# A two-layer spectral and dense network on one core: fewer filler products, the first rows in quarters, and vector work moved between steps

## The chip, the cores and the metric

The kernel runs on one core of a Trainium2 chip. The metric is the device time of one execution in microseconds (us); the median of several executions counts. The engines are PE (matmuls; its weight loads are listed as PEld), DVE (vector), ACT (activation functions, copies), POOL and SP. Each runs its own stream of instructions in order and waits for the others by semaphores. SP, ACT and POOL also issue the transfers (DMAs).

## The reference

Two kinds of layer, A and B, are applied in turn, twice: A, B, A, B. x is 2048 x 1024 in bf16.

```python
def _layernorm(x, axis=-1, eps=1e-5):
    m = jnp.mean(x, axis=axis, keepdims=True)
    v = jnp.var(x, axis=axis, keepdims=True)
    return (x - m) / jnp.sqrt(v + eps)

def _A_ref(x, w_r, w_i):                      # a filter in the frequency domain
    X = jnp.fft.rfft2(x.astype(jnp.float32), axes=(-2, -1))
    X = X * (w_r + 1j * w_i)
    return jnp.fft.irfft2(X, s=(S, D), axes=(-2, -1)).astype(jnp.bfloat16)

def _B_ref(x, w1, b1, w2):                    # w1 is 1024 x 3584, w2 is 3584 x 1024
    h = jnp.einsum("bsd,df->bsf", x, w1) + b1
    act = h * jnp.tanh(softplus(h))           # softplus is written out in full there
    return jnp.einsum("bsf,fd->bsd", act, w2)

x = x + _A_ref(_layernorm(x), A_w_r, A_w_i)
x = x + _B_ref(_layernorm(x), B_w1, B_b1, B_w2)
x = x + _A_ref(_layernorm(x), A_w_r, A_w_i)
x = x + _B_ref(_layernorm(x), B_w1, B_b1, B_w2)
```

## The kernel before, in words

x stays on the chip as `XS`, 16 tiles of 128 tokens. A Python class records each engine's instructions in the order of the calls and works out the semaphore waits; nothing is reordered. So the order in which the code calls its helpers is the order on each engine. `Res` objects keep track of who wrote and who read a buffer; a transfer that fills part of a buffer is put down to the `Res` of that part, and a reader waits for all transfers of that `Res`.

**The start.** `prologue` issues on the SP queue: the 16 tiles of x, small constants, and a second copy of x with the axes turned (`XR`), which the first stage of A reads as its stationary operand. Each of the 24 transfers of `XR` takes one eighth of the columns and some rows, in runs of 256 bytes: 8 transfers for rows 0 to 63 (`xr0`), 8 for rows 64 to 95, 8 for rows 96 to 127. Behind them on the queue are the tables `FD` and `JT`, the filter rows of the groups 0 and 1 (`load_wr`), and more tables. `first_scales` works out the scale of each token (DVE, ACT), and `scaled(j)` multiplies a constant matrix by the scales of one group of 8 row pairs, on DVE or POOL (L615) or, for j = 1, on ACT in 8 instructions (L609).

**A.** `s1` is the first stage: 16 groups of 8 matmuls (L634), four to a quarter of `XR`, each evicted by ACT (L640) or DVE (L642). Then `order_A` lists the rest of A by hand, as three-digit words: stage, group, half. Stage 2 (`s2`, L741) is a transform that ACT (L776) or DVE (L778) evicts; in the first A `filter_bins` (L1032 on PE, L1043 on DVE, L1047 on ACT) follows some of these words and prepares the filter. Stage 3 (`s3`, L786 to L789) is the next transform: ACT scales it (L798), DVE multiplies by the filter in four instructions (L800 to L807). Stages 4 and 5 (`i1`, L842, and `i2`, L872 and L904) go back; ACT evicts them (L858, L916), and the rows are written to DRAM (`u_turn`) and read back turned (`u_back`, `u_last`) for the last stage `i4` (L1071). The last rows, of group 7, are read back in four transfers, two on ACT's queue and two on SP's; a part of `i4` waits for the one that holds its rows.

While those rows travel, PE runs filler: `spin` (L651, real operands, result unused), `residual_first` (L1060, puts the old x into PSUM) and `hold` (L656), which adds n products with a zero matrix to a bank, so that the bank's value stays. `hold` is called with 16 (first A) or 11 (second A) ahead of `i4`, and once more with 2 after its first part.

**B, first product, start.** B works on four chunks of 512 tokens (4 tiles). `mm1(c, fg, half)` (L1220) multiplies chunk c, or half of it, by two blocks of 128 columns of w1: 8 matmuls each into one of three PSUM banks in rotation, which ACT evicts with Mish (L1224). Between those calls stand the residual sums of the tiles (`residual(j)`, DVE, L1498), the statistics for the layer norm, either on DVE (L470, L473) or on ACT (`stats_act`: two passes over a tile, Copy and Square, with a running sum, both L451; DVE's `sums_to_mv` from L462 on turns the sums into mean and variance), the scales, `apply` (L522, the normalised tile) and the transposes by PE (L1181) with DVE's copies (L1186).

**B, the Strassen-like parts.** The chunks 0 and 1, then 2 and 3, are multiplied by seven products each instead of eight. `quads` does that for the first matrix, one step per pair of w1 blocks: products by PE (L1260), the sums by DVE (`add`, L1265), Mish by ACT (L1270), copies of a shared product by ACT (L573, in `block`); `corner` finishes one of the quarters. After each step it calls `after(n)`, a list of things to do in step n: loads, statistics, scales, `normal(j)` (apply and transpose by DMA) and residual sums. In the second B (`last`), some blocks and corners come ahead of `quads`. `products` does the second matrix (L1359), with DVE's sums (L1402, L1410).

The layers are joined with no barrier: what one layer's last steps release is what the next layer waits for.

## Time and profile before

| what | value |
|---|---|
| median of 3 executions | 928.98 us (928.76 to 930.48) |
| the profiled execution: its own time | 925.04 us |
| its span, first to last instruction | 923.2 us |
| granted TensorE clock | 1.000 |
| PE busy | 877.7 us, 95% of the span |
| DVE, ACT, POOL busy | 623.4, 435.0, 147.7 us |
| chain that ended last, PE's share | 88% |
| costliest groups on PE | L1359 340.1 us, L1260 280.4 us, L1220 73.4 us |

In the profile a line like L1260 is the line of the kernel that issued the instruction. "ARENA" and "PS" are the on-chip buffer and PSUM, "XS" is x. A timeline line begins with the start and the duration in us; a bracket at its end is the idle time of the engine before it and what ended it. Times of the second half of the kernel are counted from the same start: the first A runs to about 117 us, the first B to 474, the second A to about 564, and the second B to the end.

### The profile page before, as it was taken

The numbers are of one execution on the slowest core, as the hardware profiler recorded it, in microseconds if no ns is written. First come the engines' busy times: TensorE is split into PE (matmuls) and PEld (weight loads), VectorE is DVE, ScalarE is ACT, GpSimd is POOL, SyncE is SP. The second block draws the span as 40 slices with busy tenths as digits, with TensorE's granted clock in tenths as the row PEclk, the third lists the DMA queues.
The fourth block names the chain that finished last, engine by engine and source line by source line (L and its number), as shares of the span: only waits on it lengthen the run. The fifth ranks groups of instructions, "written<-read, shape, count | busy, mean of one in ns | idle before, by whom it ended". The sixth has DMA issues, their size and how long they took to land.

```text
span 923.2 us, 13610 instructions
## 1 busy us (share of the span) xinstructions
PE 877.7 (95%) x5503; PEld 471.1 (51%) x5503; DVE 623.4 (68%) x995; ACT 435.0 (47%) x645; POOL 147.7 (16%) x170
## 2 busy tenths in 40 slices
PE   0899889999999999999998998999999999999998
PEld 0677576444444444444456766754444444444443
DVE  7798468686889667568767765676747655554463
ACT  7898485456203485420018966757540025552000
POOL 0732004960004651010121200000000000000000
PEclk9999999999999999999999999999999999999999
DMA  9979861575786388364723786345166645732432
GB/s 279 284 249 287 219 194 67 210 266 139 262 281 239 131 317 298 121 233 143 281 92 114 221 217 161 137 175 184 23 197 189 204 148 180 269 121 86 173 129 102
DMA packets 153502, 175.98 MB, mean 191 GB/s; under 512 B 75000, under 2 KB 132568, under 8 KB 153320
## 3 DMA queue, kind: packets, MB, share of 16 engines
q1 hardware_dynamic: 140256, 130.32, 45.9%
q0 software_dynamic: 10032, 42.90, 12.5%
q10 hardware_dynamic: 3152, 1.90, 0.7%
q8 instruction: 43, 0.70, 0.3%
q14 instruction: 19, 0.16, 0.0%
HBM read 130.78 MB, written 40.89 MB: 186 GB/s over the span
## 4 chain that ended last, share of the span: by engine, by line
PE 88%; DVE 6%; ACT 3%; SPq 2%; DMA 1%; issue 0%; DVEq 0%
PE PS L1359 37%; PE PS L1260 30%; PE PS L1220 6%; PE PS L741 3%; PE PS L842 2%; PE PS L872 2%; SPq L251 2%; PE PS L1071 2%; PE PS L634 1%; PE PS L651 1%; ACT ARENA L640 1%; PE PS L1181 1%; PE PS L904 1%; PE PS L1060 1%; ACT ARENA L451 1%; PE PS L656 1%
## 5 line engine op out<-in xcount | busy, mean ns | idle before, releaser
L1359 PE MATMUL PS<-ARENA 128*128 128x512 bf16 x1568 | 340.1, 379 | 0.0
L1260 PE MATMUL PS<-ARENA 128*128 128x512 bf16 (+1 forms) x1288 | 280.4, 379 | 0.8 <-DVE ARENA L1265 0.8
L1359 PEld LDWEIGHTS PS<-ARENA 128*128 128x128 bf16 x1568 | 153.3, 98 | 184.5
L1265 DVE TENSOR_TENSOR ARENA<-PS,ARENA 128x512 f32<-128x512 f32 x230 | 157.1, 691 | 100.2 <-PE PS L1260 92.4
L1260 PEld LDWEIGHTS PS<-ARENA 128*128 128x128 bf16 x1288 | 125.3, 98 | 153.3 <-DVE ARENA L1265 3.6
L1270 ACT ACTIVATE ARENA<-ARENA,B 128x512 bf16<-128x512 f32 x138 | 98.8, 721 | 69.1 <-DVE ARENA L1265 63.8
L573 ACT ACTIVATE ARENA<-PS 128x512 f32<-128x512 f32 (+3 forms) x86 | 61.6, 726 | 110.6 <-PE PS L1260 92.5
L1153 POOL TENSOR_TENSOR ARENA<-ARENA 128x512 bf16<-128x512 bf16 x56 | 71.5, 1278 | 74.3 <-DVE ARENA L522 61.1
L451 ACT ACTIVATE ARENA<-XS 128x1024 bf16<-128x1024 bf16 x60 | 63.2, 1053 | 36.6 <-DVE XS L1410 33.0
L1220 PE MATMUL PS<-ARENA 128*128 128x256 bf16 (+1 forms) x528 | 73.4, 295 | 3.4 <-DVE ARENA L1186 1.9
L1384 DVE TENSOR_TENSOR ARENA<-ARENA 128x3584 bf16<-128x3584 bf16 x32 | 63.9, 2017 | 0.0
L1410 DVE TENSOR_TENSOR XS<-PS,ARENA 128x512 bf16<-128x512 f32 x52 | 35.7, 689 | 39.0 <-PE PS L1359 38.7
L1220 PEld LDWEIGHTS PS<-ARENA 128*128 128x128 bf16 x528 | 50.3, 98 | 22.3 <-DVE ARENA L1186 3.3
L1402 DVE TENSOR_TENSOR ARENA<-PS,ARENA 128x512 f32<-128x512 f32 x48 | 32.9, 688 | 28.0 <-PE PS L1359 27.6
L1224 ACT ACTIVATE ARENA<-PS,B 128x256 bf16<-128x256 f32 (+1 forms) x66 | 33.0, 515 | 29.0 <-PE PS L1220 28.8
L1270 ACT ACTIVATE ARENA<-PS,B 128x512 bf16<-128x512 f32 x46 | 31.5, 685 | 18.4 <-PE PS L1260 18.4
L1398 DVE TENSOR_TENSOR ARENA<-ARENA,XS 128x512 f32<-128x512 f32 x52 | 36.8, 731 | 0.5
L442 ACT ACTIVATE RS<-MV,EPS 128x1 f32<-128x1 f32 (+2 forms) x11 | 3.3, 296 | 71.5 <-DVE MV L564 70.1
L741 PE MATMUL PS<-FD,ARENA 128*128 128x256 bf16 (+1 forms) x256 | 31.4, 271 | 2.5 <-ACT ARENA L640 2.5
L842 PE MATMUL PS<-ARENA 128*128 128x256 bf16 x256 | 32.6, 273 | 1.0 <-DVE ARENA L807 0.6
L798 ACT ACTIVATE ARENA<-PS 128x1024 bf16<-128x1024 f32 x30 | 30.4, 1046 | 5.0 <-PE PS L789 5.0
L1235 DVE TENSOR_TENSOR ARENA<-ARENA 128x2048 f16<-128x2048 bf16 x16 | 25.3, 1583 | 9.0 <-PE PS L1220 8.7
(102 smaller groups left out, 811.4 us busy)
## 6 DMA issues: line engine op xcount, KB each, us to landing
ARENA<-in_B_w_dram SPq DMA_DIRECT2D x30, 896.0 KB, 6.7
ARENA<-w1s_scratch SPq DMA_DIRECT2D x28, 896.0 KB, 4.7
ARENA<-w2s_scratch SPq DMA_DIRECT2D x24, 896.0 KB, 6.6
w1s_scratch<-ARENA POOLq DMA_DIRECT2D x14, 896.0 KB, 4.6
ARENA<-in_B_w_dram SPq DMA_DIRECT2D x24, 512.0 KB, 4.3
u_scratch<-ARENA SPq DMA_DIRECT2D x14, 512.0 KB, 4.9
ARENA<-u_scratch SPq DMA_DIRECT2D x14, 512.0 KB, 6.0
w2s_scratch<-ARENA POOLq DMA_DIRECT2D x8, 896.0 KB, 4.1
```

The lines of the kernel that those rows point to most:

```text
L451: self.op(act, lambda e, i=i, f=f: e.activation(junk.ap, x, f, accum_out=sums[:, i:i + 1]), reads=[self.r_xs[j]], writes=[junk.res], parts ...
L573: fn = (lambda e: e.activation(dst, src, ACT.Copy)) if scale is None else \
L741: fns.append(lambda e: e.matmul(dst, at(r), FD[:, t:t + n], start=start, stop=stop))
L842: fns.append(lambda e, c=c, part=part: e.matmul(ps[:, c * 256:(c + 1) * 256], yk.ap[:, part, c * P:(c + 1) * P], t[:, (128, 0)[part]:(384, ...
L1153: self.op(self.pool, lambda e, dst=A(dst), x=A(x), y=A(y), op=op: e.tensor_tensor(dst, x, y, op), reads=[b.res] + list(after), writes=[b.rs])
L1220: fns.append(lambda e, db=db, bank=bank, fl=fl: e.matmul(PS[:, bank, 0:w], wb.ap[:, db, fl * P:(fl + 1) * P], x.ap[:, db, tok], start=(db ...
L1260: self.group([lambda e, db=db: e.matmul(PS[:, bank, :], A[:, db, :], mov[:, db, :], start=(start and db == 0), stop=(db == 3), skip_group_ ...
L1265: self.op(dve, lambda e: e.tensor_tensor(dst.ap, PS[:, bank, :], x.ap, ALU.add), reads=[self.r_bank[bank], x.res], writes=[dst.res])
L1270: self.op(act, lambda e: e.activation(at, src, ACT.Mish, bias=self.B1[:, ft:ft + 1]), reads=[res, self.r_b1], writes=[ra])
L1359: self.group([lambda e, i=i, k=k, b=PB[n][k].ap: e.matmul(PS[:, bank, :], ap[:, i, t * P:(t + 1) * P], b[:, i - 7 * k, :], start=(start an ...
L1384: self.op(dve, lambda e: e.tensor_tensor(ap[dst][:, f, :], ap[x][:, f, :], ap[y][:, f, :], op), reads=part(x, k) + part(y, k), writes=part ...
L1398: self.op(dve, lambda e: e.tensor_tensor(a[t], a[t], x, ALU.add), reads=[rx], writes=[r[t]])
```

## The change

It has five parts. (1) `XR` is loaded in four quarters of 32 rows, 32 transfers instead of 24, and a group waits for its own quarter. (2) In `order_A` the word 221 moves ahead of 400. (3) `hold` ahead of `i4` runs 12 products instead of 16 in the first A, and 5 instead of 11 in the second. (4) `stats_act` can do one of its two passes; the four passes for the tiles 6 and 7, until now two after `mm1(0, 1, 1)` and two after `mm1(0, 2, 1)`, come one after each of `mm1(0, 1, 1)`, `mm1(0, 2, 1)`, `mm1(0, 3, 1)`, and the last one after `mm1(0, 4)` in the first B or after `corner(1, 4)` in the second. (5) In `quads` of the second B the residual sums of the tiles 12 and 13 are made in steps 1 and 3 instead of both in step 7; those of 14 and 15 stay in steps 8 and 9, and the first B keeps its steps.

```diff
-        for q, n in ((0, 2), (2, 1), (3, 1)):
+        for q in range(4):
             r = Res(f"xr{q}")
             for h in range(8):
-                s = slice(32 * q, 32 * (q + n))
+                s = slice(32 * q, 32 * q + 32)
                 self.dma(sp, self.XR.ap[h:P:8, s, :], xv[h][:, s, :], f"xr{q}", parts=[r])
-            self.r_xr += [r] * n
+            self.r_xr.append(r)
...
-    def stats_act(self, j):
+    def stats_act(self, j, passes=(0, 1)):
         act = self.act
         x, sums, rs, junk = self.XS[:, j, :], self.BN[:, j, 0:2], self.r_mv[j], self.junk
-        rs.begin()
-        for i, f in enumerate((ACT.Copy, ACT.Square)):
+        if passes[0] == 0:
+            rs.begin()
+        for i in passes:
+            f = (ACT.Copy, ACT.Square)[i]
...
-        self.hold(11 if li else 16, 7)
+        self.hold(5 if li else 12, 7)
...
-        order = ("200 201 210 211 300 301 220 310 400 221 311 401 230 320 410 500 231 321 411 501 330 331 420 510 240 511 421 241 "
+        order = ("200 201 210 211 300 301 220 310 221 400 311 401 230 320 410 500 231 321 411 501 330 331 420 510 240 511 421 241 "
...
         for fg in range(1, 4):
             mm1(0, fg, 1)
-            if fg < 3:
-                self.stats_act(5 + fg)
+            self.stats_act(6 + fg // 3, ((fg - 1) % 2,))
         if not last:
             mm1(0, 4)
+            self.stats_act(7, (1,))
...
             corner(1, 4)
+            self.stats_act(7, (1,))
             turns(1, 0)[0]()
...
-            for j in {first + 1: (12, 13), first + 2: (14,), first + 3: (15,)}.get(n, ()):
+            late = {1: (12,), 3: (13,), 8: (14,), 9: (15,)} if last else {5: (12, 13), 6: (14,), 7: (15,)}
+            for j in late.get(n, ()):
                 residual(j)
```

## The prediction

> **What bounds the kernel now.** I read the page first (engine shares, chain), then the waits of PE, then PE's timeline around each place that the diff touches, and last the timelines of the engine named as releaser.

> ```profile
> span 923.2 us, 13610 instructions
> ...
> PE 877.7 (95%) x5503; PEld 471.1 (51%) x5503; DVE 623.4 (68%) x995; ACT 435.0 (47%) x645; POOL 147.7 (16%) x170
> ...
> PE 88%; DVE 6%; ACT 3%; SPq 2%; DMA 1%; issue 0%; DVEq 0%
> ```

> PE is busy 95% of the span and is 88% of the chain. No edit removes useful matmuls, so all that can be won is idle time of PE, and filler that stands where PE could start real work. The waits of PE (total, times, longest, in us) name the idle time:

> ```profile
> PE PS L634 <- DMA ARENA<-in_A_x_dram: 2.7, 1, 2.7
> ...
> PE PS L1220 <- ACT ARENA L1224: 1.4, 3, 0.6
> ...
> PE PS L1260 <- DVE ARENA L1265: 0.8, 1, 0.8
> ...
> PE PS L842 <- DVE ARENA L807: 0.6, 1, 0.6
> ```

> Each of these four is the target of one edit. PE's timeline shows where they lie (start, duration; idle before and releaser in brackets), with the filler L656 of the first layer:

> ```profile
> 23.97 7.87 PE L634 MATMUL PS<-ARENA 128*128 128x128 bf16 x80 [2.73 <-DMA ARENA<-in_A_x_dram]
> ...
> 107.25 3.66 PE L656 MATMUL PS<-BD,ARENA 128*128 128x512 bf16 x16
> 110.92 0.95 PE L1071 MATMUL PS<-MT,ARENA 128*128 128x32 bf16 x32
> ...
> 139.53 2.77 PE L1220 MATMUL PS<-ARENA 128*128 128x256 bf16 x16 [0.62 <-ACT ARENA L1224]
> 142.47 3.63 PE L1220 MATMUL PS<-ARENA 128*128 128x512 bf16 x16 [0.17 <-ACT ARENA L1224]
> ...
> 498.55 1.05 PE L842 MATMUL PS<-ARENA 128*128 128x256 bf16 x8 [0.64 <-DVE ARENA L807]
> ...
> 586.83 1.05 PE L1220 MATMUL PS<-ARENA 128*128 128x256 bf16 x8 [0.61 <-ACT ARENA L1224]
> ...
> 659.48 2.76 PE L1260 MATMUL PS<-ARENA 128*128 128x512 f16 x12 [0.78 <-DVE ARENA L1265]
> ```

> Matmuls overlap, so the bracket understates what is lost; I take the start-to-start step of the matmuls (0.109 us for 256 columns, 0.216 for 512) and count what exceeds it.

> [...]The trace shows the half rate at the start (L634 steps 0.107 us from 23.97 to 29.9, then 0.056) and shows that PE keeps the full rate after a gap of 1.16 us before 38.11 and 1.30 us before 491.00 (L741 steps 0.109). [...]Mish evictions L1224 whose matmuls are done wait behind L451. [...]between 13 and 31 us the DMA share is 1.23 to 1.30 at 213 to 236 GB/s[...].

> **The change part by part.**

> *Rows in quarters.* The first half of the transposed x comes now as 8 transfers of 256 KB, the last issued at 18.67 and landing 5.2 us later, at 23.9: PE starts at 23.97. As quarters, PE needs 8 of 128 KB. The first 256 KB landed at 15.25 and the rest at some 0.62 us per 128 KB, so the first quarter is there by about 19.6 and the new bound is the scaled matrices: L615 of group 0 ends at 22.77, the 8 L609 of group 1 at 24.12. Group 1 then starts at 24.15, not 24.80: 0.65 gained. The second quarter (wait added before group 4; all later groups queue behind it on PE) should land at about 24.6, needed at 26.7. From 30.1 on, ACT's L640 evictions pace the groups, and the end of the stage moves from 38.0 to about 37.4. Then the cover ends: PE's L1032 (39.59) needs filter rows whose last transfer is issued at 32.87 on the same SP queue and lands 6.3 us later, 39.2. SP issues 8 transfers more: 16 at 0.67 instead of 8 at 1.2, about 1.1 us more in the unblocked part[...]. From 13.86 I get 26 x 0.67 = 17.4 us, to 31.3, against 31.09: 0.2 late. So L1032 could start at 39.45: a gain of 0.1. POOL's filter loads wait for the same stage (37.26), start 0.6 earlier, and compete with those rows. I take 0; bounds -0.6 (nothing late next) and +0.8 (all 1.1 us of issue felt, less 0.35 of slack before L1032).

> *Order of A.* `221` before `400`. In the second A, PE ends s3 (1,0) at 497.74 and waits for L807 until 498.55. The s2 group of 8 matmuls (0.87 us) fits there; i1 (0,0) then starts at 498.62, not before its data (498.50), and s3 (1,1) at 499.5 instead of 500.30: 0.8. The next i1 (0,1) needs DVE's second product, done at 500.5, so it starts at 500.55 and not 501.17: 0.62 remains, and PE runs without a longer wait to 539.8. On ACT the eviction of `221` goes ahead of that of `400`; the s3 eviction behind both moves up with PE. Gain 0.6, bounds 0 to 0.8. In the first A, DVE is busy without a break from 42.04 to 60.4 and paces the stage; its order is unchanged: 0.

> *Zero products.* First layer: 16 become 12, PE would be free 4 x 0.216 = 0.86 us earlier, at 110.05. But L1071 reads u rows issued by ACT at 107.51, 3.2 us to landing: 110.7. Gain 0.2; the next reads, issued at 108.17 and landing 3.7 later (111.87), just match. Second layer: 11 become 5, PE free at 557.1 instead of 558.37; rows issued at 553.82 plus 4.1 land at 557.93. Gain 0.4; the next rows (554.46 + 4.6 = 559.06) are needed at 559.2. Sum 0.6, bounds 0 and 2.15 (all 10 products).

> *Statistics of tiles 6 and 7.* Each tile is two ACT passes L451 of 1.15 us start to start. Two together hold back the Mish that frees PE's bank:

> ```profile
> 136.79 1.06 ACT L451 ACTIVATE ARENA<-XS 128x1024 bf16<-128x1024 bf16 x1
> ...
> 137.97 1.06 ACT L451 ACTIVATE ARENA<-XS 128x1024 bf16<-128x1024 bf16 x1
> ...
> 139.02 0.82 ACT L1224 ACTIVATE ARENA<-PS,B 128x256 bf16<-128x256 f32 x2
> ```

> The matmuls that this Mish evicts started at 136.13 and ended at 137.2. Five groups start every 0.87 us, the sixth is due at 138.75 and starts at 139.53: 0.78 lost. A second loss, 142.47 against 142.15, is 0.33. With one pass between two evictions, that Mish runs at 137.97 to 138.4, before the bank is needed; the later ones have 0.9 us of room. Gain 1.1. In the second layer only the sixth group is late (586.83, 0.78); one pass moves ahead of the four L573 copies, so the first copy starts at 589.25 and the second ends at 590.34, just when `corner(1)` (now 591.16, then 590.38) needs it. Gain 0.78. DVE's L462 now waits for the last pass (about 145.2 and 593.3): ahead of it stand the L1186 copies, which end at about 146.7 and 593.9, so it is not the later one; the scales and applies of tiles 6 and 7 behind it keep their distance. Sum 1.9, bounds 0.8 and 2.0.

> *Residual sums of 12 and 13.* DVE's queue before the stall at 659.48:

> ```profile
> 657.08 0.54 DVE L522 TENSOR_SCALAR FD<-XS,MV,RS 128x1024 bf16<-128x1024 bf16 x1
> 657.53 1.28 DVE L1498 TENSOR_TENSOR XS<-XS,ARENA 128x1024 bf16<-128x1024 bf16 x2
> 658.74 3.37 DVE L1265 TENSOR_TENSOR ARENA<-PS,ARENA 128x512 f32<-128x512 f32 x5
> ```

> The two sums go to steps 1 and 3, one each. Without them L1265 starts 1.2 us earlier and PE continues at 658.54: 0.94. In step 1 DVE idles 1.03 us before its five L1265 (1.11 in the step after), and one sum takes 0.65: it fits. Gain 0.9, bounds 0 and 0.95.

> Sum: 0 + 0.6 + 0.6 + 1.9 + 0.9 = 4.0 us. The profiled execution took 925.04 us (span 923.2); it would take 921.0. The median of the runs is 928.98, 3.9 above that execution; I take the same 4.0 off it: **925.0**. A difference of 0.2%, 1.9 us, is about what a measurement of this kernel can tell from no change.

> **The rivals.**

> (1) *Gains given back later.* The early gains (holds, statistics) are lost where a transfer sets the start: the second A begins after a fixed run of 31 fillers (474.19 to 480.88) with 0.21 us of idle time that no engine explains; if its rows come at a fixed time, the first layer's 1.3 us go. For it: the rows come over POOL, ACT and SP queues. Against it: those transfers are issued by the DVE work that PE's products release, so they move with PE; and the waits of PE name no DMA but the one at 23.97. With SP's extra issues at the upper bound as well (+0.8): 4.0 - 1.3 - 0.8 = 1.9, about 927.0.

> (2) *The clock falls.* The shorter holds leave PE idle before L1071, 0.7 and 0.9 us by my count. If that is enough, each layer pays what the start paid: six microseconds at half rate, 3 us of work lost, twice: 6.0 - 4.0 = 2.0 slower, 931.0.[...] Against it: PE kept its clock over 1.30 us.

> (3) *DVE becomes the bound in steps 1 and 3:* the sums delay L1265 and PE waits there instead of at step 8. It costs at most 2 x 0.65 - 0.94, so the edit would be worth -0.4: 926.3.

> **How the numbers follow.** Main case 0.73 (923 to 926.5), rival 1 0.14, rival 3 0.06, rival 2 0.07. The low end, 923.0, has every part near its upper bound without all the holds; the high end, 928.3, takes in rivals 1 and 3. Faster by over 0.2%: main, rival 3 and 0.04 of rival 1, which lies at the edge, 0.83; within 0.2%: the rest of rival 1, 0.10; slower: rival 2, 0.07.

> **What would show it.** In the changed profile: the wait of L634 on the DMA under 0.5; L1032 about where it was; the wait of L842 on L807 gone; L1071 released by a DMA after an idle PE in both layers; L1220's waits on L1224 at most 0.2; no wait of L1260 on L1265 near 655. Wrong would be L1220 steps near 120 us of twice the 0.109 (rival 2), L1032 later than 40, or a new DMA wait near 480.

## The result: no measurable change, and the profile after

The changed kernel took 929.68 us (median of 6 executions, 926.99 to 930.85) against 928.87 us for the kernel before (6 executions, 927.86 to 930.48). The ratio is 1.0003, 95% interval 0.9986 to 1.002. The forecast was a gain, to 925.0 us, range 923.0 to 928.3. No gain was measured, and the time lies 4.7 us above the forecast and 1.4 us above its range.

Gains and losses of a few microseconds each nearly cancel. I start with the page of the changed kernel, its head and the shares of the chain that ended last (lines after 446 have moved by two: L634 is now L636, L1071 is L1073, L1220 is L1222):

```profile
span 927.4 us, 13599 instructions
...
PE 878.6 (95%) x5493; PEld 473.7 (51%) x5493; DVE 623.9 (67%) x995; ACT 434.9 (47%) x645; POOL 148.3 (16%) x170
...
PE 86%; DVE 4%; SPq 3%; DMA 3%; ACT 2%; issue 1%; ACTq 0%; DVEq 0%
```

PE has ten matmuls less, as intended, and yet it is busy 0.9 us longer. The share of the chain that is neither PE nor DVE nor ACT has grown: SP's queue 2% to 3%, DMA 1% to 3%. The waits of PE (total, times, longest, in us) say which transfers:

```profile
PE PS L636 <- DMA ARENA<-ARENA: 4.2, 1, 4.2
...
PE PS L636 <- DMA ARENA<-in_A_x_dram: 2.2, 1, 2.2
PE PS L1073 <- DMA ARENA<-u_scratch: 2.0, 2, 1.6
```

The first line is new and is PE's largest wait after its first matmul. The waits of L1222 on Mish (L1226), of L1262 on DVE's sums (L1267) and of L844 on L809 are no longer in the list: three targets were hit. PE's timeline of the changed kernel shows where the waits lie (start, duration; idle before and its releaser in brackets):

```profile
22.49 1.01 PE L636 MATMUL PS<-ARENA 128*128 128x128 bf16 x8 [1.68 <-DVE ARENA L617]
...
34.78 2.84 PE L636 MATMUL PS<-ARENA 128*128 128x128 bf16 x32 [2.19 <-DMA ARENA<-in_A_x_dram]
38.80 3.15 PE L743 MATMUL PS<-FD,ARENA 128*128 128x256 bf16 x16 [1.19 <-ACT ARENA L642]
41.74 0.98 PE L1034 MATMUL PS<-ARENA 128*128 128x256 bf16 x4
...
112.86 0.95 PE L1073 MATMUL PS<-MT,ARENA 128*128 128x32 bf16 x32 [0.44 <-DMA ARENA<-u_scratch]
...
139.81 7.20 PE L1222 MATMUL PS<-ARENA 128*128 128x256 bf16 x41
...
474.91 6.85 PE L653 MATMUL PS<-BD 128*128 128x512 bf16 x31
485.95 6.24 PE L636 MATMUL PS<-M,ARENA 128*128 128x128 bf16 x77 [4.19 <-DMA ARENA<-ARENA]
...
564.19 0.95 PE L1073 MATMUL PS<-MT,ARENA 128*128 128x32 bf16 x32 [1.61 <-DMA ARENA<-u_scratch]
...
654.66 13.54 PE L1262 MATMUL PS<-ARENA 128*128 128x512 bf16 x62
```

Three lines of the kernel before, to set beside these:

```profile
38.11 1.69 PE L741 MATMUL PS<-FD,ARENA 128*128 128x256 bf16 x16 [1.16 <-ACT ARENA L640]
...
474.02 6.85 PE L651 MATMUL PS<-BD 128*128 128x512 bf16 x31
481.09 6.83 PE L634 MATMUL PS<-M,ARENA 128*128 128x128 bf16 x104 [0.21 <-issue]
```

Read the changed kernel from the top. PE starts 1.48 us earlier on its first quarter of x, then stands still for 2.19 us ahead of group 12, which needs the last quarter. The 16 matmuls of L743 take 3.15 us where they took 1.69: half rate. The stretch from 139.81 has no bracket where the old one had Mish waits, and the stretch from 654.66 none where PE waited for DVE. And the second A starts at 485.95, 11.04 us after the first of the 31 fillers, where it was 7.07 us (474.02 to 481.09).

The start of one step in the two traces gives the running balance (changed kernel minus kernel before, in us; negative is ahead; the notes are my reading of the step down to that line):

```
first product of A          22.49 - 23.97  = -1.48
first L743 / L741           38.80 - 38.11  = +0.69   last quarter late
first L844 / L842           49.55 - 46.73  = +2.82   half rate, filter rows late
first i4                   112.86 - 110.92 = +1.94   first shorter hold
first L1361 / L1359        218.02 - 217.12 = +0.90   statistics, first B
fillers before second A    474.91 - 474.02 = +0.89
second A                   485.95 - 481.09 = +4.86   new wait
second s3, L844 / L842     504.73 - 498.55 = +6.18   half rate again
last spin, second A        557.69 - 552.19 = +5.50   order of A
second i4                  564.19 - 558.21 = +5.98   second shorter hold
second L1361 / L1359       668.04 - 663.80 = +4.24   statistics, residual sums
```

So two places lose: the first 50 us (2.8) and the start of the second A (4.0, and 1.3 more at half rate). The early rows need care, for executions scatter there and the one profiled of the kernel before was early. Over the twelve traces of this document with the old loads of `XR` the first L1032 starts between 39.64 and 42.83 us, 40.7 on average; over the five with quarters between 41.74 and 43.76, 42.7 on average. By these means the quarters are 2.0 us late there.

The clock shows both losses in the table by stage, where the kernel before has 1.00 in both stretches (columns: busy time and instructions of PE, PEld, DVE, ACT, POOL; granted clock; DMA share; GB/s):

```profile
20.00:50.00 30.00, 23.62 (x206) 19.06 (x207) 21.23 (x26) 23.55 (x34) 20.62 (x20) 0.89 0.94 270
474.00:492.00 18.00, 13.81 (x113) 9.26 (x112) 7.23 (x10) 3.89 (x5) 3.19 (x6) 0.91 0.22 58
```

### The profile page after: what moved, and what is told of

Same layout as the page of the kernel before. It is cut to its first block, busy times and chain, and to the rows that moved or that the text cites. A ratio compares the mean times of both kernels' runs of the same rounds, so it can differ in the third digit from the quotient of the medians.

```text
span 927.4 us, 13599 instructions
## 1 busy us (share of the span) xinstructions
PE 878.6 (95%) x5493; PEld 473.7 (51%) x5493; DVE 623.9 (67%) x995; ACT 434.9 (47%) x645; POOL 148.3 (16%) x170
## 4 chain that ended last, share of the span: by engine, by line
PE 86%; DVE 4%; SPq 3%; DMA 3%; ACT 2%; issue 1%; ACTq 0%; DVEq 0%
PE PS L1361 36%; PE PS L1262 30%; PE PS L1222 7%; SPq L251 3%; PE PS L743 3%; PE PS L844 2%; PE PS L874 2%; PE PS L1073 2%; DMA ARENA<-u_scratch 1%; PE PS L1183 1%; ACT ARENA L642 1%; PE PS L636 1%; DMA xn_scratch<-ARENA 1%; PE PS L906 1%; PE PS L788 1%
## 5 line engine op out<-in xcount | busy, mean ns | idle before, releaser
L1262 PE MATMUL PS<-ARENA 128*128 128x512 bf16 (+1 forms) x1288 | 280.2, 379 | 0.0
L1267 DVE TENSOR_TENSOR ARENA<-PS,ARENA 128x512 f32<-128x512 f32 x230 | 157.2, 691 | 98.9 <-PE PS L1262 91.1
L1262 PEld LDWEIGHTS PS<-ARENA 128*128 128x128 bf16 x1288 | 125.6, 98 | 152.0 <-DVE ARENA L1267 2.1
L575 ACT ACTIVATE ARENA<-PS 128x512 f32<-128x512 f32 (+3 forms) x86 | 61.8, 726 | 110.7 <-PE PS L1262 92.6
L1222 PE MATMUL PS<-ARENA 128*128 128x256 bf16 (+1 forms) x528 | 72.9, 295 | 2.0 <-DVE ARENA L1188 1.9
L1222 PEld LDWEIGHTS PS<-ARENA 128*128 128x128 bf16 x528 | 50.5, 98 | 20.1 <-DVE ARENA L1188 3.3
L1226 ACT ACTIVATE ARENA<-PS,B 128x256 bf16<-128x256 f32 (+1 forms) x66 | 33.2, 515 | 28.0 <-PE PS L1222 27.8
L743 PE MATMUL PS<-FD,ARENA 128*128 128x256 bf16 (+1 forms) x256 | 32.9, 279 | 2.5 <-ACT ARENA L642 2.5
L844 PE MATMUL PS<-ARENA 128*128 128x256 bf16 x256 | 32.7, 273 | 0.3 <-DVE ARENA L831 0.3
```

Source lines behind the costliest of these rows:

```text
L575: fn = (lambda e: e.activation(dst, src, ACT.Copy)) if scale is None else \
L743: fns.append(lambda e: e.matmul(dst, at(r), FD[:, t:t + n], start=start, stop=stop))
L844: fns.append(lambda e, c=c, part=part: e.matmul(ps[:, c * 256:(c + 1) * 256], yk.ap[:, part, c * P:(c + 1) * P], t[:, (128, 0)[part]:(384, ...
L1222: fns.append(lambda e, db=db, bank=bank, fl=fl: e.matmul(PS[:, bank, 0:w], wb.ap[:, db, fl * P:(fl + 1) * P], x.ap[:, db, tok], start=(db ...
L1262: self.group([lambda e, db=db: e.matmul(PS[:, bank, :], A[:, db, :], mov[:, db, :], start=(start and db == 0), stop=(db == 3), skip_group_ ...
L1267: self.op(dve, lambda e: e.tensor_tensor(dst.ap, PS[:, bank, :], x.ap, ALU.add), reads=[self.r_bank[bank], x.res], writes=[dst.res])
```

## The experiments

Each kernel was timed beside the kernel before on the same chip, in 6 to 22 executions. Ratios are to that kernel, with the 95% interval; they are not always the ratio of the medians. The rows stand in groups of four, four, four and three, each group on its own chip, on which the kernel before had a median of 927.67, 927.91, 928.24 and 928.60 us. Across groups only the ratios compare.

| kernel | what it is | median, us | ratio |
|---|---|---|---|
| `before_again` | kernel before | 928.11 | 1.0001 (0.9987 to 1.0014) |
| `after_again` | changed kernel | 930.44 | 1.0029 (1.0019 to 1.004) |
| `halves` | changed kernel, old loads of `XR` | 928.78 | 1.0001 (0.9986 to 1.0016) |
| `quarters_only` | before with quarters | 929.78 | 1.0017 (1.0003 to 1.0032) |
| `stats_only` | before with statistics spread | 925.55 | 0.9978 (0.9966 to 0.999) |
| `holds_only` | before with shorter holds | 930.88 | 1.0031 (1.0013 to 1.005) |
| `order_only` | before with the new order of A | 928.27 | 0.9994 (0.9984 to 1.0004) |
| `residual_only` | before with residual sums moved | 928.57 | 1.0003 (0.9991 to 1.0014) |
| `spin8` | `holds_only` with 4 more fillers | 928.35 | 1.0002 (0.9992 to 1.0012) |
| `nospin` | before with 4 fillers fewer | 930.20 | 1.0019 (1.0 to 1.0038) |
| `three_edits` | order, statistics, residual sums | 924.80 | 0.9956 (0.9941 to 0.997) |
| `after_store` | changed kernel, three writes on ACT | 925.53 | 0.9967 (0.9954 to 0.998) |
| `quarters_fill` | `quarters_only` with filler in the gap | 931.59 | 1.0026 (1.0011 to 1.0041) |
| `halves_store` | `after_store`, old loads of `XR` | 924.12 | 0.9946 (0.9927 to 0.9966) |
| `best_store` | `three_edits`, first hold 12, writes on ACT | 923.51 | 0.9933 (0.9906 to 0.996) |

### The whole change again, and without its quarters

`halves` is the changed kernel with the loads of `XR` put back:

```diff
-        for q in range(4):
+        for q, n in ((0, 2), (2, 1), (3, 1)):
...
-                s = slice(32 * q, 32 * q + 32)
+                s = slice(32 * q, 32 * (q + n))
```

and `quarters_only` is the same edit the other way round, on the kernel before. `before_again` and `after_again` are unchanged copies.

> The kernel before, unchanged, for a second profile of it. Theory C (the late start of the second A, 3.9 us in the profile of the changed kernel, is chance and comes in both kernels): same time as before, and the spans of its executions scatter by some 4 us; in this profile PE may wait for the turned rows of x after the 31 fillers L651 as well, by 0 to 4 us. Rival G (the gains of the changed kernel are given back there because it comes earlier): PE's idle time after the fillers stays under 0.5 us, as in the first profile of before. Granted clock 1.000 under both.

> The changed kernel, unchanged, for a second profile of it. Theory Q (the quarters cost 2.4 us by a late last quarter and a clock that falls in the first A): PE waits about 2 us for the last quarter before group 12 and the clock falls to half for some 3 to 7 us near 36 us, again. Theory C: the wait at the start of the second A differs from the 4.2 us of the first profile, anywhere from 0 to 5. Rival G: it is 4 us again. Time within 0.3% of before.

> The changed kernel with the old loads of the turned x (a half and two quarters), all other edits kept. Theory Q with C: 3 to 4.5 us faster than before (925 against 929): the two holds 0.4 to 0.8, the order of A 0.6, the statistics 1.8, the residual sums 0.9; no wait above 0.6 us in the first stage after its start, clock full near 36 us. Rival G: at most 1 us faster than before, with PE idle for 4 us at the start of the second A. Rival N (the edits are worth nothing that can be measured): within 1 us of before.

> The kernel before with the quarters alone. Theory Q: about 2.4 us slower than before (931.3); SP's queue reaches FD 1 to 1.4 us later, PE waits some 2 us for the last quarter, and the clock falls near 36 us. The prediction's own working: 0 (within 0.8 us of before). If only the clock's fall is chance: 0.7 us slower when it does not fall.

The copy of the changed kernel came out 0.29% slower than before; the two intervals for this kernel meet at 0.19 to 0.20%, 1.8 us. The quarters cost 0.17%, 1.6 us, by themselves (interval 0.3 to 3.0 us), and taking them out of the changed kernel is worth 1.7 us by the medians (930.44 to 928.78), 2.6 by the ratios. The start of the second A was late in `after_again` (10.26 us from the first filler) and `halves` (10.72), and on time in `before_again` (7.03) and `quarters_only` (7.02). So it is not the chance of one execution, as theory C had it, and it does not come from the quarters: `halves`, from which theory Q with C expected 3 to 4.5 us, gained nothing. What rival G forecast for `halves` came in, but its cause, that the kernel comes there earlier, does not hold: `three_edits` below comes there earlier, too, and starts on time.

SP's timeline shows where the quarters' cost begins. This is the queue of the changed kernel (a group of issues of one kind to a row):

```profile
8.13 24.30 SPq L251 DMA_DIRECT2D ARENA<-in_A_x_dram  x32
32.47 0.62 SPq L251 DMA_DIRECT2D FD<-c_fd  x1
33.13 0.43 SPq L251 DMA_DIRECT2D ARENA<-c_jt  x1
33.61 0.61 SPq L251 DMA_DIRECT2D ARENA<-in_A_w_r_dram  x1
34.26 0.61 SPq L251 DMA_DIRECT2D ARENA<-in_A_w_i_dram  x1
```

This is the queue of the kernel before:

```profile
7.46 23.58 SPq L251 DMA_DIRECT2D ARENA<-in_A_x_dram  x24
31.09 0.62 SPq L251 DMA_DIRECT2D FD<-c_fd  x1
```

There 24 transfers ran to 31.04. Now 32 transfers end at 32.43, and all behind them is 1.4 us later. Half of that is the quarters': this queue also began 0.67 us later in this execution. From the first of these issues to `FD` it takes 24.34 us in place of 23.63; over all traces 24.34 to 25.08 with quarters and 23.39 to 25.20 without, 24.9 and 24.1 on average. The last quarter landed at 34.73 (33.46 before), and the first filter rows at 41.09 (39.22). In `quarters_only` the pair is 35.17 and 41.09. PE waits ahead of group 12 for 2.19 to 3.83 us in the four traces with quarters and no filler there. With the old loads it waits there too in some executions, mostly 0.5 to 1.1 us, but 2.10 in `halves` and 2.93 in `best_store`; in these two the clock fell as well, and so it did in `stats_only` after 1.13.

### One edit at a time

`stats_only`, `holds_only`, `order_only` and `residual_only` each have one of the other edits of the diff, on the kernel before.

> The kernel before with the statistics passes of tiles 6 and 7 spread, nothing else. Theory G1 (this edit is what makes the second A start late): in its profile PE idles some 4 us after the 31 fillers L651, the write of tile 10 (the last of the three that POOL issues there) takes 5 to 6 us and not 2.8, the clock falls there, and the time is 1 to 3 us over before. Theory G2 (the late start comes from another edit, or from chance): L634 follows the fillers within 0.5 us and the time is 1.9 us under before (926.0 against 927.9). In both, the waits of L1220 on L1224 are gone, 1.1 and 0.78 us.

> The kernel before with 12 and 5 products in the two holds, nothing else. Theory K[...]: the mean number of stretches at half clock rises from 0.65 to 1.2 or more, most of them just after the second hold, each costs 1.5 us, and the time is 0 to 1 us over before. The prediction's working: 0.6 us under before, clock unchanged.

> The kernel before with 221 ahead of 400 in the list of A, nothing else. The prediction's working: 0.6 us under before, all of it in the second A (L1071 there 0.6 earlier, first A unchanged), granted clock as before. Theory K: PE is busier, so no stretch more at half clock. Theory G3 (this edit makes the second A start late): PE idles some 4 us after the 31 fillers.

> The kernel before with the residual sums of tiles 12 and 13 in steps 1 and 3 of the second B, nothing else. The prediction's working: 0.9 us under before, no wait of L1260 on L1265 in step 8 of that part. Rival 3 of the prediction (DVE becomes the bound in steps 1 and 3): 0.4 us over before, PE waits there. Clock as before under both, and no late start of the second A, which comes earlier in the program.

Statistics gained 0.22%, 2.0 us. The order of A has a ratio 0.06% under before, 0.6 us, the forecast's figure, but its interval takes in zero, and its median is not under that of the kernel before. The residual sums did not show in the time (+0.3 us, interval -0.8 to +1.3), though in their trace the step from PE's first product of the quads to L1359 of the second B shrank from 53.99 to 53.04 us.

The holds, forecast as a gain, cost 0.31%, 2.9 us. Theory K, that the shorter holds bring stretches at half clock, was half right: the mean granted clock was 0.9965 against 0.9988 beside it, about 1.9 stretches at half rate an execution against 0.65, but in the trace they lie at the start of the second A, not behind the second hold, and the loss is larger than it forecast. PE's timeline of `holds_only`, at the start of the second A:

```profile
473.42 6.85 PE L651 MATMUL PS<-BD 128*128 128x512 bf16 x31
484.13 8.08 PE L634 MATMUL PS<-M,ARENA 128*128 128x128 bf16 x94 [3.86 <-DMA ARENA<-ARENA]
```

The wait of the changed kernel is there with this edit alone, 10.71 us after the first filler; the other three had 7.23 to 8.15. Yet the edit that can act there stands 360 us earlier, in the first A, and its gain is real: from the last of the residual products L1060 to `i4` 3.06 us, where it was 4.10.

What starts the second A is a relay. POOL writes the tiles 8, 9 and 10 to `xn_scratch` in DRAM, SP reads each back turned when its write has landed, and direct copies of tile 11 stand behind those reads on the same queue. The waits of SP's queue between 464 and 486 us, first in the changed kernel and then in the kernel before:

```profile
SPq L251 <- DMA xn_scratch<-ARENA: 15.6, 3, 9.3
```

```profile
SPq L251 <- DMA xn_scratch<-ARENA: 11.4, 3, 6.7
```

The difference is 4.2 us, the length of PE's new wait. The three writes took 3.2, 4.8 and 2.8 us to land before, and 4.8, 2.8 and 6.0 in the changed kernel. The first lands late, so the read of tile 8 starts at 471.04 with the read of tile 9 right behind it at 472.26, and both run while the third write is trying to get through. That one lands at 478.54 (474.49 before), the read of tile 10 starts then, and the last direct copy lands at 486.20 in place of 482.40. The copy that released PE went out at 480.49, behind that read, and took 5.11 us. That the reads hold back the third write is inferred from their order; what the traces show is that it takes 5.5 to 6.0 us in the five late ones and 2.8 or 2.9 in the others in which POOL issues it.

Why is the first write late? The transfers of the changed kernel, from its first data packet to its landing (the strip has 40 equal slices; rows below are queue, kind, packets, MB, share of the 16 engines):

```profile
DMA  9959989810000000000030000200010100000189
GB/s 386 434 241 530 386 337 434 289 48 0 0 0 0 0 0 0 0 0 0 0 48 0 0 0 0 48 0 0 0 48 0 48 0 0 0 0 0 48 337 386
...
q0 software_dynamic: 96, 0.33, 25.8%
q8 instruction: 1, 0.02, 3.2%
```

The bulk has passed after 8 slices of 0.085 us. The rest trickles through, one packet to a slice (48 GB/s for 0.085 us is 4 KB); what holds it back no view shows. In the same window lies one transfer of 16 KB of the kind "instruction", which starts 1.48 us after the write's issue and takes 1.77 us. In the kernel before it lies between the issue and the first packet at +1.47, where the queues are empty (the transfers from 465.3 to 466.8 us, all of them):

```profile
DMA packets 1, 0.02 MB, mean 11 GB/s; under 512 B 0, under 2 KB 0, under 8 KB 0
...
q8 instruction: 1, 0.02, 3.9%
```

There it starts at +0.76 and takes 0.93 us. In `holds_only` it starts at +1.48 and takes 1.59. The page of the changed kernel counts 43 such transfers, and PE has 10,986 matmul and load instructions, 255 for each; counted in the trace, PE begins 252 of them in the middle from the start of one such transfer to the next (250 in the kernel before). So I read these transfers as fetches of PE's own program, which is inferred from the counts. Where the one of interest falls fits that: it starts when PE has begun its 2,722nd to 2,724th weight load in 16 of the 17 traces, at whatever time that comes (465.4 to 470.3 us); the other, `quarters_fill`, has 40 loads more ahead of it. Four products are eight instructions; with eight fewer ahead of it, a fetch falls four products, 0.86 us, later in the work, which is about the shift seen (+0.76 to +1.48).

### More and fewer instructions, with and without the holds

Theory F says that the place of the fetch makes the second A late; rival S says that the shorter hold does it in some other way. `spin8` keeps the shorter holds and adds four products of another kind (L651) ahead of the first `i4`. `nospin` keeps the old holds and takes the first A's four fillers of that kind away. First the edit of `spin8`, on `holds_only`, then that of `nospin`, on the kernel before:

```diff
-        self.spin(4, 0)
+        self.spin(4 if li else 8, 0)
```

```diff
-        self.spin(4, 0)
+        if li:
+            self.spin(4, 0)
```

`after_store` lets ACT, not POOL, issue the writes of the tiles 8 to 10, and `three_edits` leaves out quarters and holds:

```diff
-    def xn_store(self, j, b):
+    def xn_store(self, j, b, prog=None):
...
-        self.dma(self.pool, self.xn_d[j].rearrange("h n l -> n h l"), b.ap.rearrange("n (h l) -> n h l", l=P), f"xw{b.res.name[2:]}",
+        self.dma(prog or self.pool, self.xn_d[j].rearrange("h n l -> n h l"), b.ap.rearrange("n (h l) -> n h l", l=P), f"xw{b.res.name[2:]}{'a' if prog else ''}",
...
-                    self.xn_store(j, b)
+                    self.xn_store(j, b, act if n == 6 else None)
```

> holds_only with four more zero products of another line in the first order of A (8 in place of 4), so that TensorE's stream has as many instructions ahead of the second A as before, while both holds stay at 12 and 5. Theory F (the late start of the second A comes from where the 16-KB instruction fetch falls in the stream: with 8 instructions fewer ahead of it, it runs beside the packets of the write of tile 9's neighbour and makes that write late): no late start, 7 to 7.5 us from the last filler of the spin at 474 us to the second A's first product, the write of tile 10 in about 2.8 us, the fetch 0.6 to 0.8 us after the write's issue; time within 1 us of before. Rival S (the shorter hold itself, by an earlier turn of everything behind it): late start as in holds_only, 10.3 to 11.0 us, time about 930.5.

> The kernel before (holds 16 and 11) without the four zero products of the other line in the first order of A: 8 instructions fewer on TensorE ahead of the second A, with no change of a hold. Theory F: late start of the second A, 10.3 to 11.0 us from the last filler to its first product, the write of tile 10 in 5 us or more, the instruction fetch at about +1.5 us of the write's issue; time 929.5 to 931. Rival S: start as before, 7 to 7.5 us, and time within 1 us of before, or up to 0.9 us shorter for the four products left out.

> The change without its quarters and without its shorter holds: order of A, statistics and residual sums alone. From the single edits (statistics 2.2 us less, residual sums 0.95 us less at their place in the trace, order of A 0.6 us less): 924.2, between 923.5 and 926, start of the second A 7 to 7.7 us after the last filler. If the sums of single edits do not add (theory N: each place only waits for the same transfer later), 925.5 to 928.

> The changed kernel with the writes of tiles 8 to 10 to xn_scratch issued by ScalarE in place of GpSimd. If the late start of the second A is due to those writes being late (theory F and rival S alike): the late start goes, 7 to 8 us in place of 10.7, and the time is 2.5 to 3.5 us under the changed kernel's, 926 to 927.5. If it is due to the loads or to the direct copies of tile 11 alone: start stays at 10 us or later, time 929 to 931.

Theory F's forecasts came in, but for the two starts, each up to 0.3 us later than its band. PE's timeline of `nospin`, where no hold was touched:

```profile
474.40 6.85 PE L651 MATMUL PS<-BD 128*128 128x512 bf16 x31
485.46 6.76 PE L634 MATMUL PS<-M,ARENA 128*128 128x128 bf16 x82 [4.20 <-DMA ARENA<-ARENA]
```

and of `spin8`, with the short holds and the instruction count of before:

```profile
476.73 6.85 PE L651 MATMUL PS<-BD 128*128 128x512 bf16 x31
484.48 6.83 PE L634 MATMUL PS<-M,ARENA 128*128 128x128 bf16 x104 [0.90 <-DMA ARENA<-ARENA]
```

11.06 us against 7.75. The fetch started at +1.26 in `nospin`, and its third write took 5.5 us; in `spin8` the figures are +0.66 and 2.9. In time `nospin` lost 0.19%, 1.8 us (interval 0.0 to 3.5), for taking filler out, and `spin8` won back what `holds_only` had lost. Rival S is out: eight instructions of PE in the first A decide, in a hold or in another filler. The four products are also 0.86 us of PE's time, but the time alone does not sort the traces: the first write was issued at 464.75 to 468.56 us in the late ones and at 464.78 to 470.60 in those on time in which POOL issues it.

The link between the count and the late write is the fetch, as far as traces can show it. In the five late traces it starts 1.26 to 1.71 us after the issue of the first write, and that write takes 4.1 to 4.8 us. In eight of the nine on time in which POOL issues the writes it starts at +0.58 to +0.77, and the first write takes 3.2 to 3.5. The ninth is `quarters_fill` below: with 80 instructions of PE more the fetch falls 4.5 us ahead of the issue, and the write takes 2.8. No run moved a fetch with nothing else changed.

In `after_store` the writes took 2.3, 4.6 and 2.5 us, and the second A started 6.99 us after the first filler, with no wait at all:

```profile
475.04 6.85 PE L653 MATMUL PS<-BD 128*128 128x512 bf16 x31
482.03 2.16 PE L636 MATMUL PS<-M,ARENA 128*128 128x128 bf16 x33
```

Its ratio of 0.9967 lies 0.36% and 0.62% under the two results of the changed kernel, 3.3 and 5.8 us, on both sides of the 4.2 us of the wait that is gone. `three_edits` gained 0.44%, 4.1 us (interval 2.8 to 5.5); the forecast's terms for these edits sum to 3.4, inside it.

### The quarters' cost, and whether the parts add up

The clock fell after the gap ahead of group 12, so its half rate could be the quarters' price (theory K), or the late transfers themselves (theory Q). `quarters_fill` fills the gap with work:

```diff
+            if not li and j == 12:
+                again = [lambda e, q=q, ps=ps: e.matmul(ps[:, q * P:(q + 1) * P], XR.ap[:, 88 + q, :], self.MN.ap[:, 88 + q, :],
+                                                        start=True, stop=True) for q in range(8)]
+                self.group(again * 5, reads=[self.r_xr[2], self.r_mn[11]], writes=banks)
             self.group(fns, reads=[self.r_xr[j // 4], self.r_m if li else self.r_mn[j]], writes=banks)
```

`halves_store` and `best_store` are made of the edits above; `best_store` has `self.hold(11 if li else 12, 7)`.

> The quarters alone, with 40 products of group 11 done again ahead of group 12 of the first stage, in the time in which PE waits for the last quarter (2.9 us in quarters_only); their result is written over. If the clock's fall is what the quarters cost (theory K): no stretch at half clock between 32 and 45 us, and the time falls from 929.8 to 927.5 to 928.3, no more than 0.5 above before. If the late rows themselves cost it (theory Q): the stretch may go, L1032 still starts 1 to 1.5 us later than before (40.6 to 41.2), and the time is 928.7 to 929.5.

> The changed kernel with XR in its old three parts and with the writes of tiles 8 to 10 on ScalarE. If the parts add up: after_store (925.5) less the quarters' 1.8, 923.7, between 922.8 and 924.6; start of the second A 7 to 8 us after the last filler. If they do not (theory N): 924.8 or more, no better than three_edits.

> three_edits with 12 in place of 16 zero products in the first A only (the second keeps 11) and the writes of tiles 8 to 10 on ScalarE. By the parts: 924.8 less 0.4 to 1.0 for the first hold, 923.8 to 924.4, within 0.5 of halves_store, since the second hold was found to be worth nothing. If the second hold is worth its 0.4 (prediction), halves_store is 0.4 or more faster than this one.

PE's timeline of `quarters_fill` (its filler is L637; L1036 is the old L1032, L745 the old L741):

```profile
32.77 2.41 PE L637 MATMUL PS<-ARENA 128*128 128x128 bf16 x40 [0.30 <-ACT ARENA L644]
36.24 1.51 PE L634 MATMUL PS<-ARENA 128*128 128x128 bf16 x24 [1.07 <-DMA ARENA<-in_A_x_dram]
...
39.85 1.69 PE L745 MATMUL PS<-FD,ARENA 128*128 128x256 bf16 x16 [1.18 <-DVE ARENA L646]
42.93 0.62 PE L1036 MATMUL PS<-ARENA 128*128 128x256 bf16 x4 [1.39 <-DMA ARENA<-in_A_w_i_dram]
...
47.24 0.38 PE L791 MATMUL PS<-ARENA 128*128 128x512 bf16 x1 [1.48 <-DMA ARENA<-c_ft]
```

The clock held: L745 takes 1.69 us. But L1036 starts at 42.93, and in `quarters_only`, at half rate, L1032 started at 42.91. With the full rate PE only waits for filter rows and tables instead. Over its 22 executions, too, the mean clock was back at 0.9984, where `quarters_only` had 0.9958, and yet the time did not fall: the ratio is 1.0026 against 1.0017, with intervals that overlap. That is against theory K as the price of the quarters, and at 931.59 it missed theory Q's own forecast of 928.7 to 929.5 as well. In this execution SP's issue of `FD` also took 2.17 us (0.62 otherwise), so the rows landed 1.8 us later still than in `quarters_only`. And the filler ends near 35.2 whether or not the quarter has come, so it would delay an execution in which the quarter came earlier. How the quarters' 1.6 us divide between late rows and half rate therefore stays open.

The parts add up otherwise: `halves_store` came out at 924.12, expected 923.7. `best_store`, at 923.51, is 0.67% under the kernel before (0.40% to 0.94%), and not measurably slower than `halves_store`, which shortens the second hold too: that hold shows no gain, though with these intervals one of the forecast's 0.4 us would not show either. `best_store` is faster than the kernel before, and its interval lies below those of both results of the changed kernel.

## Why the prediction was wrong, point by point

**Zero products** (forecast 0.6 gained) is the step that failed most: it measured 2.9 us lost, 3.5 us apart. Its own arithmetic was half right. The first hold gave 0.4 us in the changed kernel (3.66 from the last L1062 to `i4`) and 1.0 in `holds_only`, for 0.2 forecast; the second gave nothing (from the last spin to `i4` 6.50 after, 6.02 before), since the rows it waits for set the time, as the new wait on `u_scratch` of 1.61 shows. What the step left out is what a shorter program moves elsewhere: the start of the second A, 4.0 us later. I counted fillers only as time on PE. The four of the first A are also eight instructions, and the 16 KB transfers of the kind "instruction" lie 252 of PE's instructions apart in the middle; the relay of writes and reads before the second A had its quiet moment just where one of them fell (+0.76 us, against +1.48 in the changed kernel). That the count decides is shown by `nospin` and `spin8`; that the fetch carries it is inferred. Two of the prediction's own signs of being wrong came: a new DMA wait near 480, and the first L1034 later than 40, at 41.74 (a weak sign, since with the old loads its average is 40.7).

**Quarters** (forecast 0) measured 1.6 us lost, twice the 0.8 that I had as the worst ("all 1.1 us of issue felt, less 0.35"), though the interval takes that in. The term that was mis-sized is SP's lateness: 0.2 forecast, 1.38 between the two traces, of which 0.67 is the later start of the queue; counted from the first issue it is 0.7, and 0.8 by the averages over all traces. I had assumed that the same bytes pass during the slow first issues (0.69, 2.50 and 3.07 us in the kernel before): six quarter-size transfers by 13.86, where three half-size ones had gone. In the trace four had gone by 13.68, so 28 were left and not 26, and 28 x 0.67 = 18.8 ends at 32.4. The same bytes did not pass: 0.5 MB in place of 0.75. A single issue is short beside its transfer, 0.67 us against 2.9 to landing; but 32 in a row took 24.3 us and set when the last quarter went out. The step also left out the half rate that PE's wait for that quarter can bring. The gain at the start was right (PE began 1.48 us earlier, group 1 at 23.75, forecast 24.15), and was gone by group 12. I followed the second quarter to its landing, and not the fourth.

**Rival 1** named the place of the loss, the second A's start, and the release by rows that come over three queues. It priced only the gains that could be lost there (1.3). The wait was 4.2 us and is no gain given back: it is new. My argument against it, that the transfers move with PE, holds for their issue, not for how long they take.

**Rival 2, the clock.** I looked for it at the holds alone. In the changed kernel the clock fell after 2.19 us ahead of group 12, at 35.68, and again after 4.19 us, at 486.24; at the holds it did not fall. In three other traces with the shorter second hold it did, for one stretch of 3.41 us each: `halves` at 565.06 (PE idle for 2.18 us ahead of `i4`), `spin8` at 564.59 (2.12) and `halves_store` at 558.65 (1.66). So this rival was right in part. The runs give no one length of gap that decides: the clock fell after 1.13 us in `stats_only`, and in the kernel before it stayed full after 1.30 us ahead of 491.00. In `after_again` the mean granted clock was 0.9943 against 0.9988 beside it. One stretch loses half of 3.41 us, so that is (1 - 0.9943) x 929 / 1.71 = 3.1 stretches an execution against 0.65. In the two places of loss the idle time came first; the clock added to it.

**Statistics** (1.9 forecast, 2.0 measured alone), **order of A** (0.6 forecast, 0.7 in the changed kernel's trace, 0.6 by `order_only`'s ratio, which is not clear of zero) and **residual sums** (0.9 forecast, 0.95 in the trace, not seen in the time alone) were right, and together measured 4.1. Rival 3 did not occur: in `residual_only` and in the changed kernel PE runs the 244 products of the quads without a wait.

The median of the runs as the base was no error of note: the profiled execution of before, 925.04, was a short one, and I took the gain off the median. The sum with the two corrections, 925.0 + 3.5 + 1.6 = 930.1, lies between the two results of the changed kernel, 929.68 and 930.44.

## What to carry to other kernels

Cutting a load into more transfers bought an earlier first part here and paid for it with the last part and everything behind it on the issuing queue; count the issues as well as the bytes, and follow the last part, not only the first. Filler that costs little where it stands can hold a later, tightly spaced relay of transfers in place; after any change of the instruction count, compare the start of each later stage that waits for a DMA. A write that must land before a read can be issued is a fragile start for a stage: here another issuing engine for three writes was worth 3.3 to 5.8 us, and the four fillers of the first A saved at most 1.0.
